# The last numerators' block split over the two column halves of TensorE, and the numerators' PSUM tiles in other banks

## The chip, the cores and the metric

The kernel runs on one core of a Trainium2 chip. The metric is the device time of one execution in microseconds (us), as the median of several executions. The engines are named as in the profile: PE is TensorE, PEld its weight loads, DVE VectorE, ACT ScalarE, POOL GpSimd (PoolE), SP SyncE with its DMA queue.

## The reference

There are 2048 tokens of width 576 and 32 heads of 18 columns. Two linear attentions run over the same input; a gate that depends on the token mixes their outputs.

```python
x = A_x
g = sigmoid((x * gate_w).sum(-1, keepdims=True))
return g * A(x) + (1 - g) * B(x)

# A: q, k, v = x @ wqkv;  phi(t) = where(t > 0, t + 1, exp(t)) + 1e-6
# B: q, k, v = x @ wqkv;  q and k times w_phi, head by head;  phi(t) = [softmax(t), softmax(-t)]
# both, head by head:
kv  = phi(k)^T v                    # summed over all tokens
z   = phi(k) summed over all tokens
o   = (phi(q) kv) / (phi(q) z + 1e-6)
out = o (heads side by side) @ wo
```

All is float32. The phi(q) kv of B is called the numerators below: its denominators and the gate are multiplied into phi(q) ahead of it.

## The kernel before

**Three stages.** First come A's keys and values, then (to about 296 us) B's. Both take the tokens in 8 pairs of tiles of 128 rows and gather the sums kv and z. A's kv is multiplied into its output weights, so A's rows need no numerators of their own. The last stage goes over the 8 pairs once more. Iteration `i` of its loop (L1292) holds the q products of pair `i + 1` (`q_units`, seven products by Strassen's scheme, into double banks), the transposes of pair `i` (`tr_units`), and the numerators (`num`) and the output (`out_units`) of pair `i - 1`. The numerators of the eight groups stand in iterations 1 to 8.

**Transposes.** For each tile of a pair, the odd one first, TensorE transposes four 128x128 pieces of A's normalised rows (`f2` of `norm_a`, profile name `row`) into one bank. ScalarE rounds them to the high part `ath`, VectorE subtracts that from the bank and writes the low part `atl` (profile: `at`). The fourth piece is columns 448 to 575 of the row. Only columns 512 to 575 of it, transposed rows 64 to 127, are used; rows 0 to 63 are overwritten later. Then the 11 blocks of B's rows (`late`) are transposed into three banks, and ScalarE copies them into `uT`, 118 x 11 x 256 for the pair.

**Numerators.** Heads go in threes: 11 blocks of up to 64 columns. A block's matmul (`kb[:, b]` against `uT[:, b]`) gives 64 rows by 256 tokens. Blocks 2n and 2n+1 are put in the lower and the upper 64 columns of the array; two such pairs fill one PSUM bank of 512 columns, so the blocks take a first tile (0 to 3), a second (4 to 7) and half of a third (8 to 10). Block 10 stands alone in the lower half; its 64 rows go into the free rows 0 to 63 of `ath[:, 3]` and `atl[:, 3]`, so that one operand of 128 rows holds both A's last rows and block 10. The other blocks go into `vo` (`oh` high, `ol` low), again by a ScalarE copy and a VectorE subtraction for each tile.

**Output.** `out_units` makes each tile's rows in two halves of 288 columns. A half is 27 matmuls into one ordinary bank: nine of A's rows, fifteen of the `vo`, and last three of the shared operand `ath[:, 3]`, `atl[:, 3]`. Its weights stand in `WOt`, loaded by `load_out` from DRAM (`WO_d`, `MA_d`) over SP's queue.

**PSUM.** All tiles come from pools of two buffers: `pq`, double banks for the products; `tr`, one bank each, for transposes; `bk`, one "ordinary" bank each, for output and other sums. The numerators before take both `tr` banks and one `bk` (`num`, L1228), and in the last two groups a `pq` and a `tr`.

**The order of the work.** Nothing is issued as it is written. `Plan` records every operation, and so in the profile all have the line L354. `weigh` gives each an estimated cost by its engine and size; `order` gives TensorE's operations due times in the order of the code, and the others due times by what they feed, which includes the operations that wait for a PSUM or SBUF buffer to come free; `run` goes through a modelled time and takes on each engine, among the operations ready, the one due first. A change of a tile's pool therefore changes the order on all engines. All matmuls of `num` are one piece and are not torn apart. A matmul with 64 output rows or fewer has another mode in this model, and a change of mode a price.

Of the kernel before, what the change touches and what calls it, by code (L numbers as in the profile page):

```python
# [13 lines left out]
F32R = mybir.dt.float32r  # L14
AF = mybir.ActivationFunctionType
ALU = mybir.AluOpType
AX = mybir.AxisListType

P = 128
S, D, H, DH = 2048, 576, 32, 18  # L20
NT = S // P
# [7 lines left out]
UB = 6 * DH + 10  # L29
NB = len(GRP3)  # L30
# [328 lines left out]
def tile_gated_mix(ctx, tc, xT, wAk, wAv, wBv, wAq, wkT, wqT, phi, woA, woB, out):  # L359
    nc = tc.nc  # L360
    plan = Plan()
    V, A, G, PE, SP = [Engine(plan, k, x) for k, x in (("DVE", nc.vector), ("ACT", nc.scalar), ("POOL", nc.gpsimd),
                                                       ("PE", nc.tensor), ("SP", nc.sync))]
# [3 lines left out]
    wk = Pool(plan, "wk", ctx.enter_context(tc.tile_pool(name="wk", bufs=2)), 2)  # L367
# [4 lines left out]
    def r(ap):  # L372
        return ap.bitcast(F32)
# [7 lines left out]
    def tr_tile():  # L381
        return ps.tile([P, 512], F32, name="tr")
# [12 lines left out]
    def bank_tile():  # L395
        return ps.tile([P, 512], F32, name="bk")

    def row_tile():
        return wk.tile([P, 612], F32, name="row", bufs=8)

    def uw_tile():
        return wk.tile([P, 2, D], F32, name="uw")

    def op_tile(w=D):
        return wp.tile([P, 4, w], F32R, name="op", bufs=11)

    def tail_tile(w=D):
        return wp.tile([P, 2, w], F32R, name="tail")
# [39 lines left out]
    kb = cst.tile([UB, NB, 64], F32, name="kb")  # L448
# [248 lines left out]
    def ub_blocks(ub):  # L697
        return ub[:, :UB * 10].rearrange("p (b c) -> p b c", c=UB)
# [101 lines left out]
    def plain(x, w1, w2, k, t, make):  # L800

        acc = make()
        xa, xb, xt = (x["11"], x["12"], x["t1"]) if t == 0 else (x["21"], x["22"], x["t2"])
        st = op_steps(xa, WA[w1]) + op_steps(xb, WA[w2]) + tail_steps(xt, TA[:, k])
        return acc, [(acc, hf, HG, st, lo, hi) for lo, hi in ((0, 3), (3, 6), (6, 9), (9, 12), (12, 14)) for hf in range(2)]
# [31 lines left out]
    for t in range(2):  # L837
        v, s = plain(x, 12, 3, 1, t, two_banks if t == 0 else pq_tile)
# [5 lines left out]
    for t in range(2):  # L844
        k, s = plain(x, 1, 2, 0, t, two_banks if t else pq_tile)
# [4 lines left out]
    for t in range(2):  # L850
        v, s = plain(x, 12, 3, 1, t, two_banks if t else pq_tile)
# [61 lines left out]
    WO_d = dr.tile([P, 6, 2, D], F32, name="wod")  # L913
# [133 lines left out]
    for n in range(NT // 2):  # L1047
        done, pend = pend, []
        if n % 2:
            lo = wk.tile([P, 2, D], F32, name="st", bufs=1) if n == 1 else area[0][:, :2 * D].rearrange("p (s n) -> p s n", s=2)  # L1050
# [24 lines left out]
    def load_out(k, at):  # L1075
        t = op_tile() if k < 4 else tail_tile()
        WOt[k] = t
        plan.first = at
        if k < 3:
            SP.dma_start(r(t).rearrange("p (i s) n -> p i s n", i=2), WO_d[:, 2 * k:2 * k + 2])  # L1080
        elif k == 3:
            to = r(t).rearrange("p (i s) n -> p i s n", i=2)
            SP.dma_start(to[:126], MA_d[:252].rearrange("(g p) s n -> p g s n", g=2))
            SP.dma_start(to[126:], MA_d[570:574].rearrange("(g p) s n -> p g s n", g=2))
        else:
            SP.dma_start(r(t[:126]), MA_d[252:378])
            SP.dma_start(r(t[126:]), MA_d[574:])

    WOt = {}

    def WO(s, i):
        return WOt[i // 2][:, 2 * (i % 2) + s]
# [36 lines left out]
    def norm_a(t, f, ub):  # L1129
        zw = row_tile()[:, :D]  # L1130
        G.tensor_tensor(zw, f[:, :D], z_a, op=ALU.mult)
        den = sm.tile([P, 32], F32, name="den")
        V.tensor_reduce(den, zw.rearrange("p (h d) -> p h d", d=DH), op=ALU.add, axis=AX.X)
        V.tensor_scalar(den, den, EPS, gate[:, 0, at_row(t):at_row(t) + 1], op0=ALU.add, op1=ALU.mult)
        V.reciprocal(den, den)

        f2 = row_tile()
        blocks = f2[:, :384].rearrange("p (g c) -> p g c", g=3)
        G.tensor_tensor(blocks[:, :, :126].rearrange("p g (k d) -> p g k d", d=DH),
                        f[:, :378].rearrange("p (g k d) -> p g k d", g=3, d=DH),  # L1140
                        den[:, :21].rearrange("p (g k) -> p g k", g=3)[:, :, :, None].to_broadcast([P, 3, GH, DH]), op=ALU.mult)
        G.tensor_tensor(f2[:, 384:582].rearrange("p (k d) -> p k d", d=DH), f[:, 378:D].rearrange("p (k d) -> p k d", d=DH),
                        den[:, 21:, None].to_broadcast([P, 11, DH]), op=ALU.mult)
        A.activation(blocks[:, :, 126:], f2[:, 576:582].rearrange("p (g c) -> p g c", g=3), AF.Copy)
        A.activation(ub_blocks(ub)[:, :, 108:], f2[:, 384:484].rearrange("p (b c) -> p b c", c=10), AF.Copy)
        A.activation(ub[:, UB * 10 + 72:UB * NB], f2[:, 484:530], AF.Copy)
        return f2

    def norm_b(t, uw, rs, ub, engs):
# [17 lines left out]
    def at_row(t):  # L1167
        return 2 * pairs[t // 2] + t % 2
# [49 lines left out]
            A.activation(uT[:UB, 4 * q:4 * q + nb, c], p1[:UB, :P * nb].rearrange("p (j n) -> p j n", n=P), AF.Copy)  # L1218
            yield

    def num(uT, at, last):
        ath, atl = at
        oh, ol = ot = [wk.tile([P, KT, 256], F32R, name="vo") for _ in range(2)]
        if last:
            q = pq_tile()
            pms = [q[:, 0], q[:, 1], tr_tile()]
        else:
            pms = [tr_tile(), tr_tile(), bank_tile()]  # L1228
        with plan.piece():
            for b in range(NB):  # L1230
                a, k = b % 2, b // 2 % 2
                PE.matmul(pms[b // 4][64 * a:64 * a + 64, 256 * k:256 * k + 256], kb[:, b, :], uT[:UB, b, :], start=True, stop=True,
                          skip_group_check=True)
        for m, p1 in enumerate(pms):
            j = 2 * m
            n = 2 if j < 4 else 1
            src = p1[:, :256 * n].rearrange("p (j n) -> p j n", n=256)
            A.activation(oh[:, j:j + n], src, AF.Copy)
            V.tensor_tensor(ol[:, j:j + n], src, r(oh[:, j:j + n]), op=ALU.subtract)
            if n == 1:  # L1240
                A.activation(ath[:64, 3], p1[:64, 256:], AF.Copy)
                V.tensor_tensor(atl[:64, 3], p1[:64, 256:], r(ath[:64, 3]), op=ALU.subtract)
        return ot

    def out_units(t, blk):
        ath, atl = blk["at"]
        oh, ol = blk["ot"]
        c = slice(P * (t % 2), P * (t % 2) + P)
        osb = row_tile()[:, :D]
        dst = out[P * at_row(t):P * at_row(t) + P]  # L1250
        for hf in range(2):
            po = bank_tile()
            cc = slice(HB * hf, HB * hf + HB)
            srcs = [(ath, atl, m, 6 + m) for m in range(3)] + [(oh, ol, j, j) for j in range(KT)] + [(ath, atl, 3, 5)]
            st = []
            for hi, lo, j, i in srcs:
                st += [(hi[:, j, c], WO(0, i)), (hi[:, j, c], WO(1, i)), (lo[:, j, c], WO(0, i))]
            for i, (l, w) in enumerate(st):
                PE.matmul(po[:, :HB], l, w[:, cc], start=(i == 0), stop=(i == len(st) - 1))
            A.activation(osb[:, cc], po[:, :HB], AF.Copy)  # L1260
            if t >= NT - 2:
                SP.dma_start(dst[:, cc], osb[:, cc])
            if hf == 0:
                yield
        if t < NT - 2:
            SP.dma_start(dst, osb)
        yield
# [16 lines left out]
    uT = wide_tile(0, [NB, 256])  # L1284
# [7 lines left out]
    for i in range(NT // 2 + 1):  # L1292
        while norms:
            norms.pop(0)()
        cur, prev = blocks[i], blocks[i - 1]
        seqs = []
        if i and i <= NT // 2:
            prev["ot"] = num(uT, prev["at"], i >= NT // 2 - 1)
        if i + 1 < NT // 2:
            x = x_fetch(pairs[i + 1])  # L1300
            if i == 0:
                load_out(3, x["dma"])
                load_out(4, x["dma"])
            if i == 1:
                for k, m in enumerate((1, 4, 6)):
                    load_out(k, x["dma"][m:m + 1])
            uws = [extra_uw if i == 0 else uw_tile(), uw_tile()]
            seqs.append((7, .7, q_units(i + 1, x, uws, row_tile)))
        ts = (2 * i + 1, 2 * i)
        if i < NT // 2:  # L1310
            at = at_tile([2, 4, 256], F32R)
            cur["at"] = (at[:, 0], at[:, 1])
            seqs.append((8, 1, chain(*[tr_units(t, cur["at"], uT) for t in ts])))
        if i:
            seqs.append((4, 1, chain(*[out_units(t, prev) for t in (2 * i - 1, 2 * i - 2)])))
        merge(*seqs)
# [86 lines left out]
```

## Time and profile before

| | |
|---|---|
| median of 3 runs | 561.73 us (561.55 to 562.09) |
| profiled execution, its own time | 561.08 us |
| its span | 559.4 us |
| granted TensorE clock | 1.0 |
| data moved by DMA | 96.22 MB, 172 GB/s over the span |
| starts of the second to the eighth numerators | 347.28, 381.94, 415.98, 450.01, 484.06, 518.10, 539.84 us |
| TensorE in 340 to 360 us | busy 19.33 of 20 us |
| TensorE in 360 to 380 us | busy 20.00 of 20 us |

Times in the trace count from the start of the span. A row of the timeline has the start, the duration, the engine, the operation with its tiles (out<-in), for matmuls the part of the array, shape, type and count, and in brackets the idle time before it and what ended it. A row of the groups has the busy time, the mean of one in ns, and the idle time before. A row of the page's first part has an engine's busy time.

### The profile page before, as it was taken

The page shows a single profiled execution, that of the slowest core. Times are in us where ns is not written, and L with a number is a line of the kernel's source. Part 1 is how long each engine was busy: PE and PEld are TensorE (multiplying, and loading weights), DVE is VectorE, ACT ScalarE, POOL GpSimd, SP SyncE. Part 2 cuts the span into 40 slices and gives each one's busy share as a digit, 9 for nine tenths or more (in the row PEclk, how much of TensorE's full clock was granted, in tenths as well). Part 3 has the DMA queues.
Part 4 walks back from the last instruction along what each step waited for, and adds up shares of the span by engine and source line. Part 5 has one row for each costly group of instructions (what it writes and reads, how often), then busy time and mean ns, then how long its engine had stood idle before and what let it go on. Part 6 is the DMA issues. An engine that isn't in the chain of part 4 may idle for free.

```text
span 559.4 us, 11694 instructions
## 1 busy us (share of the span) xinstructions
PE 550.0 (98%) x4584; PEld 525.1 (94%) x4584; DVE 423.3 (76%) x674; ACT 287.1 (51%) x602; POOL 243.7 (44%) x218
## 2 busy tenths in 40 slices
PE   9999999999999999999999989999999999999997
PEld 8999999999999978999998989998999989899897
DVE  5882678933887898998889998769597795978810
ACT  6766677655645544543355645445453544535421
POOL 6584486533783523353138764224152332424200
PEclk9999999999999999999999999999999999999999
DMA  8839677976769566887559622132322213100001
GB/s 290 283 121 332 212 261 260 353 236 256 259 243 374 169 218 217 246 248 269 209 184 312 233 88 69 51 105 68 107 79 86 98 49 117 52 2 22 33 33 42
DMA packets 38625, 96.22 MB, mean 172 GB/s; under 512 B 4198, under 2 KB 7782, under 8 KB 37034
## 3 DMA queue, kind: packets, MB, share of 16 engines
q1 hardware_dynamic: 38570, 95.47, 50.3%
q8 instruction: 36, 0.59, 0.4%
q14 instruction: 19, 0.16, 0.1%
HBM read 59.64 MB, written 36.70 MB: 172 GB/s over the span
## 4 chain that ended last, share of the span: by engine, by line
PE 77%; DVE 14%; POOL 3%; ACT 2%; issue 2%; DMA 1%; SPq 0%; POOLq 0%; ACTq 0%; DVEq 0%
PE pq L354 32%; PE tr L354 24%; PE bk L354 22%; DVE row L354 3%; DVE den L354 2%; DVE dd L354 2%; DVE ss L354 2%; DVE mm L354 1%; DVE at L354 1%; POOL late L354 1%; ACT row L354 1%; DMA at<-xT 1%; POOL row L354 1%; DVE rs L354 1%; DVE uw L354 1%
## 5 line engine op out<-in xcount | busy, mean ns | idle before, releaser
L354 PE MATMUL pq<-op,x 128*128 128x288 f32 (+1 forms) x636 | 102.4, 296 | 0.0
L354 PEld LDWEIGHTS pq<-op,x 128*128 128x128 f32 x636 | 90.1, 188 | 0.9 <-issue 0.4
L354 PE MATMUL bk<-op,vo 128*128 128x288 f32 x480 | 71.0, 297 | 0.0
L354 PE MATMUL pq<-tail,x 128*128 128x288 f32 (+1 forms) x308 | 67.2, 301 | 0.4 <-POOL x L354 0.4
L354 PEld LDWEIGHTS bk<-op,vo 128*128 128x128 f32 x480 | 65.8, 188 | 0.2 <-DVE vo L354 0.2
L354 PE MATMUL pq<-op,xp 128*128 128x288 f32 (+1 forms) x336 | 54.0, 297 | 0.0
L354 PE MATMUL bk<-op,at 128*128 128x288 f32 x288 | 51.3, 301 | 0.0
L354 PEld LDWEIGHTS pq<-tail,x 128*128 128x128 f32 x308 | 49.1, 188 | 1.9 <-POOL x L354 0.6
L354 POOL TENSOR_TENSOR row<-row,z_a 128x576 f32<-128x576 f32 x16 | 22.9, 1429 | 63.2 <-issue 35.7
L354 ACT ACTIVATE row<-bk 128x288 f32<-128x288 f32 x38 | 15.6, 410 | 64.3 <-PE bk L354 64.3
L354 ACT ACTIVATE row<-tr 128x288 f32<-128x288 f32 (+1 forms) x74 | 30.1, 408 | 34.8 <-PE tr L354 33.6
L354 PEld LDWEIGHTS pq<-op,xp 128*128 128x128 f32 x336 | 47.5, 188 | 0.2
L354 ACT ACTIVATE row<-row,epsc 128x576 f32<-128x576 f32 x54 | 41.9, 776 | 11.0 <-DVE row L354 10.1
L354 POOL TENSOR_TENSOR row<-row,den 128x378 f32<-128x378 f32 (+1 forms) x32 | 24.6, 788 | 47.8 <-DVE den L354 39.4
L354 DVE TENSOR_REDUCE ss<-uw 128x64 f32<-128x1152 f32 x23 | 31.0, 1350 | 19.0 <-ACT uw L354 18.4
L354 PEld LDWEIGHTS bk<-op,at 128*128 128x128 f32 x288 | 41.7, 189 | 0.4 <-issue 0.4
L354 POOL TENSOR_TENSOR x<-at,x 128x384 fp32r<-128x384 f32 (+2 forms) x35 | 31.6, 907 | 16.5 <-ACT x L354 15.0
L354 ACT ACTIVATE uw<-uw 128x1152 f32<-128x1152 f32 x23 | 26.8, 1164 | 21.3 <-DVE uw L354 11.1
L354 DVE TENSOR_TENSOR row<-row,pq 128x576 f32<-128x576 f32 (+1 forms) x30 | 22.5, 750 | 19.1 <-ACT row L354 14.3
L354 PE MATMUL tr<-op,xv 128*128 128x288 f32 (+1 forms) x204 | 33.6, 301 | 0.0
L354 ACT ACTIVATE uT<-tr 118x512 f32<-118x512 f32 (+1 forms) x48 | 25.9, 558 | 14.6 <-PE tr L354 14.5
L354 POOL TENSOR_TENSOR uw<-uw,rs 128x1152 f32<-128x1152 f32 x8 | 18.0, 2250 | 32.5 <-DVE rs L354 26.3
(206 smaller groups left out, 1263.3 us busy)
## 6 DMA issues: line engine op xcount, KB each, us to landing
xp<-s0x SPq DMA_DIRECT2D x12, 512.0 KB
at<-xT SPq DMA_DIRECT2D x18, 320.0 KB
x<-x1x SPq DMA_DIRECT2D x12, 384.0 KB
x<-s2x SPq DMA_DIRECT2D x12, 384.0 KB
s0x<-xp SPq DMA_DIRECT2D x8, 512.0 KB
out<-row SPq DMA_DIRECT2D x14, 288.0 KB
op<-wb SPq DMA_DIRECT2D x3, 1152.0 KB
wod<-op SPq DMA_DIRECT2D x3, 1152.0 KB
```

The costliest lines, as they stand in the source:

```text
L354: fn(*[a.real() if isinstance(a, View) else a for a in args], **{k: v.real() if isinstance(v, View) else v for k, v in kw.items()})
```

## The change

Block 10 now stands in both halves of the array: two matmuls of 128 columns (tokens) each in place of one of 256. The odd tile of a pair, which has the upper 128 tokens, finds its block 10 in PSUM rows 64 to 127, and so in rows 64 to 127 of `ath[:, 3]`. A's last rows must then stand in rows 0 to 63 there: PoolE copies columns 512 to 575 of an odd tile's normalised row to 448 to 511 ahead of the transposes, and the last three output matmuls of an odd tile take weights with the two halves exchanged, which two further loads (`load_swap`) bring into the tile `st` once. The copy and the subtraction of block 10 are made for each half.

Independent of this, the second of the three numerator tiles comes from the ordinary banks in place of the transposes' from the second group on; the first group and the last two keep the banks they had.

```diff
+    def load_swap():
+        t = WOt["swap"] = wk.tile([P, 2, D], F32R, name="st", bufs=1)
+        for a in range(2):
+            SP.dma_start(r(t[64 * a:64 * a + 64]), WO_d[64 - 64 * a:P - 64 * a, 5])
...
     def norm_a(t, f, ub):
...
+        if t % 2:
+            G.tensor_copy(f2[:, 448:512], f2[:, 512:576])
         return f2
...
-    def num(uT, at, last):
+    def num(uT, at, last, first):
...
-            pms = [tr_tile(), tr_tile(), bank_tile()]
+            pms = [tr_tile(), tr_tile() if first else bank_tile(), bank_tile()]
         with plan.piece():
-            for b in range(NB):
+            for b in range(NB - 1):
                 a, k = b % 2, b // 2 % 2
                 PE.matmul(pms[b // 4][64 * a:64 * a + 64, 256 * k:256 * k + 256], kb[:, b, :], uT[:UB, b, :], start=True, stop=True,
                           skip_group_check=True)
+            for a in range(2):
+                PE.matmul(pms[2][64 * a:64 * a + 64, 256:384], kb[:, NB - 1, :], uT[:UB, NB - 1, P * a:P * a + P], start=True, stop=True,
                           skip_group_check=True)
...
             if n == 1:
-                A.activation(ath[:64, 3], p1[:64, 256:], AF.Copy)
-                V.tensor_tensor(atl[:64, 3], p1[:64, 256:], r(ath[:64, 3]), op=ALU.subtract)
+                for a in range(2):
+                    h, c = slice(64 * a, 64 * a + 64), slice(P * a, P * a + P)
+                    A.activation(ath[h, 3, c], p1[h, 256:384], AF.Copy)
+                    V.tensor_tensor(atl[h, 3, c], p1[h, 256:384], r(ath[h, 3, c]), op=ALU.subtract)
...
     def out_units(t, blk):
...
-                st += [(hi[:, j, c], WO(0, i)), (hi[:, j, c], WO(1, i)), (lo[:, j, c], WO(0, i))]
+                w0, w1 = [WOt["swap"][:, s] if i == 5 and t % 2 else WO(s, i) for s in range(2)]
+                st += [(hi[:, j, c], w0), (hi[:, j, c], w1), (lo[:, j, c], w0)]
...
-            prev["ot"] = num(uT, prev["at"], i >= NT // 2 - 1)
+            prev["ot"] = num(uT, prev["at"], i >= NT // 2 - 1, i == 1)
...
             if i == 1:
                 for k, m in enumerate((1, 4, 6)):
                     load_out(k, x["dma"][m:m + 1])
+                load_swap()
```

TensorE's order at the third numerators (381.94 us in the profile before). `tr<-uT,kb` and `bk<-uT,kb` are numerator blocks by the bank that they go to, `pq<-op,xu` and `pq<-op,x` q products, `tr<-ident,row` the transposes of A's next rows, and `bk<-op,at`, `bk<-tail,at`, `bk<-op,vo` the first output half. Before:

```order
L354 MATMUL tr<-ident,late 118x128 x3
L354 MATMUL pq<-op,xu 128x288 x8
L354 MATMUL tr<-uT,kb 64x256 x8
L354 MATMUL bk<-uT,kb 64x256 x3
L354 MATMUL pq<-op,xu 128x288 x4
L354 MATMUL bk<-op,at 128x288 x6
L354 MATMUL bk<-tail,at 128x288 x3
L354 MATMUL bk<-op,vo 128x288
L354 MATMUL tr<-ident,row 128x128 x4
L354 MATMUL bk<-op,vo 128x288 x14
```

And now, with `bk<-st,at` for the swapped weights:

```order
L354 MATMUL tr<-ident,late 118x128 x3
L354 MATMUL pq<-op,xu 128x288 x8
L354 MATMUL tr<-uT,kb 64x256 x4
L354 MATMUL bk<-uT,kb 64x256 x6
L354 MATMUL bk<-uT,kb 64x128 x2
L354 MATMUL pq<-op,xu 128x288 x4
L354 MATMUL tr<-ident,row 128x128 x4
L354 MATMUL pq<-op,x_4581 128x288 x6
L354 MATMUL bk<-op,at 128x288 x6
L354 MATMUL bk<-tail,at 128x288 x3
L354 MATMUL bk<-op,vo 128x288 x15
L354 MATMUL bk<-st,at 128x288 x3
```

The transposes of the next rows have moved ahead of the output, six q matmuls too, and the output half is no longer torn.

VectorE's order at the same numerators: `vo<-tr,vo` and `vo<-bk,vo` are the subtractions of the numerator tiles, `at<-bk,at` those of block 10, `at<-tr,at` that of A's transposed rows. Before:

```order
L354 TENSOR_REDUCE den<-row 128x32
L354 TENSOR_TENSOR vo<-tr,vo 128x512 x2
L354 TENSOR_TENSOR vo<-bk,vo 128x256
L354 TENSOR_TENSOR at<-bk,at 64x256
L354 TENSOR_SCALAR den<-den,gate 128x32
L354 RECIPROCAL den<-den 128x32
L354 TENSOR_TENSOR row<-uw,z_b 128x576
L354 TENSOR_TENSOR at<-tr,at 128x4x128
L354 TENSOR_REDUCE dd<-row 128x32
```

Now:

```order
L354 TENSOR_REDUCE den<-row 128x32
L354 TENSOR_TENSOR vo<-bk,vo 128x512
L354 TENSOR_TENSOR vo<-tr,vo 128x512
L354 TENSOR_TENSOR vo<-bk,vo 128x256
L354 TENSOR_TENSOR at<-bk,at 64x128
L354 TENSOR_SCALAR den<-den,gate 128x32
L354 RECIPROCAL den<-den 128x32
L354 TENSOR_TENSOR row<-uw,z_b 128x576
L354 TENSOR_TENSOR at<-tr,at 128x4x128
L354 TENSOR_TENSOR at<-bk,at 64x128
L354 TENSOR_REDUCE dd<-row 128x32
```

The ordinary bank's tile is subtracted first, and the second half of block 10 stands behind the subtraction of the next transposes.

VectorE's order ahead of the second numerators' first subtraction: `dd`, `den` and `rs` are the small sums and factors of B's denominators, `row<-uw,z_b` a product with z. Before:

```order
L354 TENSOR_TENSOR dd<-dd,rs 128x64
L354 SCALAR_TENSOR_TENSOR den<-dd 128x32
L354 RECIPROCAL den<-den 128x32
L354 SCALAR_TENSOR_TENSOR rs<-den,gate,rs 128x64
L354 TENSOR_TENSOR late<-uw,rs 128x10x54 x2
L354 TENSOR_TENSOR late<-uw,rs 128x72
L354 TENSOR_REDUCE den<-row 128x32
L354 TENSOR_SCALAR den<-den,gate 128x32
L354 RECIPROCAL den<-den 128x32
L354 TENSOR_TENSOR vo<-tr,vo 128x512 x2
```

Now:

```order
L354 TENSOR_TENSOR late<-uw,rs 128x72
L354 SCALAR_TENSOR_TENSOR row<-row 128x576
L354 TENSOR_TENSOR row<-uw,z_b 128x576
L354 TENSOR_REDUCE dd<-row 128x32 x2
L354 TENSOR_REDUCE den<-row 128x32
L354 TENSOR_SCALAR den<-den,gate 128x32
L354 RECIPROCAL den<-den 128x32
L354 RECIPROCAL rs<-ss 128x64
L354 TENSOR_TENSOR dd<-dd,rs 128x64
L354 SCALAR_TENSOR_TENSOR den<-dd 128x32
L354 RECIPROCAL den<-den 128x32
L354 TENSOR_TENSOR vo<-bk,vo 128x512
```

A product with z, its reduction and the chain up to the reciprocal of the next tile now stand ahead of the subtraction.

More of the change, by code (lines that the diff above doesn't have):

```diff
@@ L1227, in num @@
         else:
-            pms = [tr_tile(), tr_tile(), bank_tile()]
+            pms = [tr_tile(), tr_tile() if first else bank_tile(), bank_tile()]
         with plan.piece():
-            for b in range(NB):
+            for b in range(NB - 1):
                 a, k = b % 2, b // 2 % 2
                 PE.matmul(pms[b // 4][64 * a:64 * a + 64, 256 * k:256 * k + 256], kb[:, b, :], uT[:UB, b, :], start=True, stop=True,
+                          skip_group_check=True)
+            for a in range(2):
+                PE.matmul(pms[2][64 * a:64 * a + 64, 256:384], kb[:, NB - 1, :], uT[:UB, NB - 1, P * a:P * a + P], start=True, stop=True,
                           skip_group_check=True)
```

## The prediction

> **What bounds the kernel now.** I read the page first: how busy each engine is, and the chain that ended last.
>
> ```profile
> PE 550.0 (98%) x4584; PEld 525.1 (94%) x4584; DVE 423.3 (76%) x674; ACT 287.1 (51%) x602; POOL 243.7 (44%) x218
> ...
> PE 77%; DVE 14%; POOL 3%; ACT 2%; issue 2%; DMA 1%; SPq 0%; POOLq 0%; ACTq 0%; DVEq 0%
> ```
>
> TensorE is busy for 550.0 of 559.4 us and carries 77% of the chain. So a change counts if it shortens TensorE's stream or changes the few places where TensorE stands still. Next I read TensorE's timeline around one of the eight numerator groups, the third. The start time comes first, then the duration; an x16 stands for 8 matmuls, each issued in two records.
>
> ```profile
> 381.94 1.95 PE L354 MATMUL tr<-uT,kb 118*64 118x256 f32 x16
> 383.71 1.03 PE L354 MATMUL bk<-uT,kb 118*64 118x256 f32 x6
> 384.67 0.81 PE L354 MATMUL pq<-op,xu 128*128 128x288 f32 x4
> 385.32 0.95 PE L354 MATMUL bk<-op,at 128*128 128x288 f32 x6
> 386.11 0.56 PE L354 MATMUL bk<-tail,at 128*128 128x288 f32 x3
> 386.51 0.29 PE L354 MATMUL bk<-op,vo 128*128 128x288 f32 x1
> 386.85 0.63 PE L354 MATMUL tr<-ident,row 128*128 128x128 f32 x4
> 387.23 2.10 PE L354 MATMUL bk<-op,vo 128*128 128x288 f32 x14
> ...
> 389.57 0.96 PE L354 MATMUL pq<-op,x 128*128 128x288 f32 x6
> ...
> 391.69 0.60 PE L354 MATMUL tr<-ident,late 128*118 128x128 f32 x4
> ```
>
> Eight blocks take 383.71 - 381.94 = 1.77 us, 0.44 per pair of blocks: a pair's two matmuls run side by side in the two column halves. The three blocks of the second row take 384.67 - 383.71 = 0.96, so the last block, alone in its half, costs about 0.96 - 0.44 = 0.52 with the way back to the whole array. The transposes at 386.85 start 0.34 after the matmul before them, where 0.13 is usual (six from 385.32 to 386.11): 0.2 us is lost. The weight loads say the same, and VectorE's timeline says why.
>
> ```profile
> 386.82 0.42 PEld L354 LDWEIGHTS tr<-ident,row 128*128 128x128 f32 x4 [0.25 <-issue]
> ```
>
> ```profile
> 383.82 1.62 DVE L354 TENSOR_TENSOR late<-uw,rs 128x540 f32<-128x540 f32 x3
> 385.36 0.74 DVE L354 TENSOR_REDUCE den<-row 128x32 f32<-128x576 f32 x1
> 386.02 1.28 DVE L354 TENSOR_TENSOR vo<-tr,vo 128x512 fp32r<-128x512 f32 x2
> ...
> 387.55 0.40 DVE L354 TENSOR_TENSOR at<-bk,at 64x256 fp32r<-64x256 f32 x1
> ```
>
> VectorE is busy without a gap until it subtracts the first two numerator tiles from 386.02 on; the first of these ends near 386.66, and 0.16 later the transposes get its bank. So the release stands at 4.88 us after the group's start (386.82 - 381.94), set by VectorE's queue and not by TensorE. The longer stops of TensorE in this stage, and the start of the second group:
>
> ```profile
> 302.65 1.09 PE L354 MATMUL tr<-ident,late 128*118 128x128 f32 x8 [0.63 <-POOL late L354]
> ...
> 325.08 0.66 PE L354 MATMUL tr<-ident,row 128*128 128x128 f32 x4 [1.16 <-DVE vo L354]
> 333.96 1.09 PE L354 MATMUL tr<-ident,late 128*118 128x128 f32 x8 [0.32 <-POOL late L354]
> ...
> 347.28 1.95 PE L354 MATMUL tr<-uT,kb 118*64 118x256 f32 x16
> ...
> 352.67 0.63 PE L354 MATMUL tr<-ident,row 128*128 128x128 f32 x4 [0.67 <-DVE vo L354]
> ...
> 522.41 0.54 PE L354 MATMUL tr<-ident,late 128*118 128x128 f32 x3 [0.79 <-DVE at L354]
> ```
>
> **The last block in two halves.** Two matmuls of 128 columns, one in each array half, replace one of 256. The trace has no 64-wide matmul of 128 columns; the nearest are those that gather the k-v sums, mostly 108 columns wide, also alternating between the halves:
>
> ```profile
> 281.75 2.31 PE L354 MATMUL bk<-at,vo 128*55 128x108 f32 x44
> 283.98 1.08 PE L354 MATMUL tr<-op,xv 128*128 128x288 f32 x6
> ```
>
> That is 2.23/44 = 0.051 us per record. Scaled by 128/108 it is 0.060, and four records take 0.24 where the lone block streams for about 0.43 to 0.44 (a pair's time): I take 0.2 off each group, bounds 0 (the halves do not overlap) and 0.22 (exactly half a pair). TensorEngine Tiling (Array Packing) in the Trainium skill, section Performance Considerations, gives column tiling up to 2x for a stationary width of at most 64; by this alone the sum would be 8 x 0.2 = 1.6 us less.
>
> **The banks, third to sixth group.** From the second group on, the numerators hold one bank of the transposes and both ordinary banks. The transposes of the next rows therefore have a free bank and lose their wait; the output's first tile, which used to start right behind the group, now needs an ordinary bank that VectorE must first empty. The new order puts four transposes and six q matmuls in front of it and has VectorE subtract the ordinary bank's tile first. Nothing on VectorE before that subtraction is moved in this group, so the release stays at 4.88. TensorE's arrival: the group 2.73 - 0.2 = 2.53 (384.67 - 381.94), four q matmuls 0.65, four transposes 0.38 (387.23 - 386.85), six q matmuls about 0.8: 4.36. It waits 0.5 us. Before, at the same release, it had done the group, four q and ten output matmuls (0.65 + 10 x 0.133 = 1.98 behind the group); now it has done 0.65 + 0.38 + 0.8 = 1.83 behind it. What is then left is 391.69 - 386.85 = 4.84 in the one and 27 output and 10 q matmuls at 0.133 = 4.92 in the other. So the next transposes come 0.05 to 0.1 us later; I take **+0.05 per group, +0.2 for four**. The saving of the halves drops out, since TensorE waits for the same subtraction anyway. If VectorE were early it would be worth -0.4 each (0.2 of stream and 0.2 of the lost wait), the lower end. PSUM Bottleneck, a section of the same page of the Trainium skill, warns that tiling speeds TensorE but not the emptying of PSUM; the rows above bear it out here, and by it this term is zero or above.
>
> **Smaller evictions.** The last block's two evictions become four of half the width.
>
> ```profile
> L354 DVE TENSOR_TENSOR at<-bk,at 64x256 fp32r<-64x256 f32 x6 | 2.4, 407 | 0.0
> L354 DVE TENSOR_TENSOR row<-bk,row 55x108 f32<-55x108 f32 x2 | 0.5, 264 | 0.0
> L354 DVE TENSOR_TENSOR row<-bk,row 55x36 f32<-55x36 f32 x2 | 0.4, 192 | 0.0
> ...
> L354 ACT ACTIVATE at<-bk 64x256 fp32r<-64x256 f32 x6 | 2.2, 366 | 0.0
> ```
>
> From 192 ns at 36 and 264 at 108 columns, 128 columns cost about 0.28 on VectorE: 0.57 for two in place of 0.41, so +0.16; ScalarE between 0 and +0.37. They lie behind the subtraction that TensorE waits for. One counts: the odd tile's half is subtracted after the next transposes' tile, and the last matmul of the first output tile needs it. That matmul is due at 4.88 + 26 x 0.133 = 8.3 after the group's start. VectorE gets there after 4.08 + 1.2 + 0.33 + 0.28, two small operations (0.5), a product 0.67, the transposes' tile 0.6 and the half itself 0.28 = 7.9. The cover is 0.3 to 0.4 us; beyond it the excess is paid once per group.
>
> **First and second group.** The first keeps its banks: TensorE arrives 0.2 earlier and waits for the same subtraction, so it gains nothing. Behind it the planner has moved the output's rest behind the q matmuls, and VectorE's second subtraction behind a reduction. The second group is decided on VectorE:
>
> ```profile
> 328.26 0.75 DVE L354 TENSOR_TENSOR row<-uw,z_b 128x576 f32<-128x576 f32 x1
> 328.93 1.41 DVE L354 TENSOR_REDUCE dd<-row 128x32 f32<-128x576 f32 x2
> 330.37 0.23 DVE L354 TENSOR_TENSOR dd<-dd,rs 128x64 f32<-128x64 f32 x1
> ...
> 331.24 0.28 DVE L354 SCALAR_TENSOR_TENSOR rs<-den,gate,rs 128x64 f32<-128x64 f32 x1
> ...
> 340.92 1.35 DVE L354 TENSOR_REDUCE ss<-uw 128x64 f32<-128x1152 f32 x1 [1.50 <-ACT uw L354]
> ...
> 342.85 1.55 DVE L354 TENSOR_TENSOR row<-uw,z_b 128x576 f32<-128x576 f32 x1
> ...
> 351.90 1.22 DVE L354 TENSOR_TENSOR vo<-tr,vo 128x512 fp32r<-128x512 f32 x2
> ```
>
> By the new order one more product with z_b (0.67 to the next start), one reduction (0.72) and a chain of three small ones (330.37 to 331.24: 0.87) come before the second group's first subtraction: 2.26 us. The idle 1.50 at 340.92 can take the most of it up, and the product that was stretched to 1.55 may run in 0.75. So the subtraction starts between 351.9 and 352.7, and the output's tile 0.8 later, at 352.7 to 353.5, with as much work done as before at 352.67: 0 to +0.8. If VectorE did not bind, TensorE would come by itself at 347.28 + 4.36 = 351.6, -1.0. I take **+0.2**, near the early end, since the waits on PoolE and ScalarE also move up.
>
> **Copy, swapped weights, last groups.** PoolE's new copies (8 x 128x64) stand behind the two products with z_b:
>
> ```profile
> 377.13 3.37 POOL L354 TENSOR_TENSOR row<-uw,z_b 128x576 f32<-128x576 f32 x2 [0.45 <-ACT uw L354]
> ```
>
> ```profile
> masks.py:197 POOL MEMSET ident<- 128x128 f32 x1 | 0.2, 197 | 0.0
> ```
>
> Between 0.1 and 0.4 us each, by the nearest row 0.2. They end near 380.7, and the transposes that need them come at 385.1: covered by 4 us. Only in the first rows (about 299) TensorE meets the copy; that wait takes the place of the 0.63 at 302.65: **+0.1**, from 0 to 0.3. The two loads of the swapped weights stand on SyncE ahead of this load:
>
> ```profile
> 281.85 0.32 SPq L354 DMA_DIRECT2D x<-s1x  x1
> ```
>
> ```profile
> 300.66 1.36 PE L354 MATMUL bk<-op,x 128*128 128x288 f32 x9
> ```
>
> It lands later by their two issues, some 0.7, with 18 us before the matmuls that read it: nothing. The seventh group's 0.2 goes into the wait at 522.41, which is for a subtraction that comes before: 0. Behind that row TensorE stops no more, so the eighth group keeps its saving: **-0.2**.
>
> Sum: 0.1 + 0.2 + 0.2 + 0 - 0.2 = +0.3. The profiled execution took 561.08 (its span 559.4 and 1.68 around it); 561.4 on it. The runs' median, 561.73, is 0.65 above that execution: **562.0 us**. A measurement of this kernel can tell 0.2%, 1.1 us, from no change.
>
> **Rivals.** *The saving arrives (faster).* VectorE releases the ordinary bank 0.4 us earlier than worked out, or the waits hide elsewhere. Then third to sixth give 4 x -0.4, the second -0.5, the eighth -0.2, with +0.1: -2.2, 559.5. For it: the old waits are all on the transposes' banks, which the change frees. Against it: VectorE's rows have no gap before 386.02. Chance 0.21. The 2x of the tiling page points the same way, though by that page alone it would be -1.6.
>
> *The odd half comes late (slower).* The last matmul of the first output tile stands for the second half's subtraction, queued behind the next transposes' tile. It decides from VectorE reaching it 8.2 us or more after the group's start; my margin is 0.3. At 0.7 later it costs 0.4 in each of the second to sixth groups, +2.0, and with the +0.3: 564.0. For it: these are the fullest stretches of VectorE. Against it: the margin. Chance 0.28.
>
> *The halves do not overlap.* Then each group is as long as before; only the eighth shows it: +0.2, 562.2, within the forecast's class. Chance 0.04.
>
> **How the numbers follow.** The forecast, no change within 1.1 us, has the remaining 0.47, with the overlap rival 0.51. Its own range takes the bounds: -1.0 to +0.8 in the second group, 0 to 0.3 at the copy, about 0.2 per group on the four: 560.8 to 563.0. For 8 in 10 I reach into both others, 560.2 to 563.6. Faster 0.21, same 0.51, slower 0.28.
>
> **What would show it.** Right: the numerators' last four records within 0.3 us; no wait before the transposes of the next rows; a wait of 0.3 to 0.6 at the first output tile in the third to sixth groups, released by VectorE; periods of 34.0 to 34.2 us from group to group. Wrong: no such wait and periods of 33.6 (first rival), or a stop at the first output tile's last matmul (second). A stop in front of the second group's output beyond 0.8, or a late load at 300, would break the sum elsewhere.

## The result and the profile after

The changed kernel takes 563.14 us in the median of 6 runs (562.21 to 563.86), the kernel before 561.64 beside it. The ratio is 1.0031, with a 95% interval of 1.0019 to 1.0042. So it is slower, by 1.5 us between the medians and 1.7 by the ratio. The time lies inside the predicted range of 560.2 to 563.6, but just above the 560.8 to 563.0 that the prediction's own terms allowed, and its likeliest case was no change.

The page after, busy times and the chain that ended last:

```profile
PE 550.8 (98%) x4600; PEld 527.0 (94%) x4600; DVE 425.5 (76%) x682; ACT 287.6 (51%) x610; POOL 249.8 (44%) x226
...
PE 65%; DVE 24%; ACT 4%; issue 3%; POOL 3%; DMA 1%; SPq 0%; POOLq 0%; ACTq 0%; DVEq 0%
```

TensorE has as much work as before within 0.8 us; VectorE's share of the chain has grown from 14% to 24%. TensorE's timeline in the first two groups:

```profile
315.83 1.95 PE L354 MATMUL tr<-uT,kb 118*64 118x256 f32 x16
...
325.69 0.66 PE L354 MATMUL tr<-ident,row 128*128 128x128 f32 x4 [1.38 <-DVE vo L354]
...
331.28 0.40 PE L354 MATMUL bk<-op,vo 128*128 128x288 f32 x1 [1.21 <-DVE vo L354]
...
334.72 1.09 PE L354 MATMUL tr<-ident,late 128*118 128x128 f32 x8 [0.25 <-POOL late L354]
...
349.25 1.08 PE L354 MATMUL tr<-uT,kb 118*64 118x256 f32 x8
...
354.24 1.05 PE L354 MATMUL bk<-op,at 128*128 128x288 f32 x6 [0.42 <-DVE vo L354]
```

The stop of 1.21 us at 331.28 is new. From the first to the second group it now takes 33.42 us (349.25 - 315.83), and took 32.04 (347.28 - 315.24). The matmul that stops reads the first group's third numerator tile. VectorE's timeline after shows when that tile is subtracted, and the row behind it where it stood before:

```profile
326.81 0.68 DVE L354 TENSOR_TENSOR vo<-tr,vo 128x512 fp32r<-128x512 f32 x1
327.40 1.76 DVE L354 TENSOR_TENSOR row<-uw,z_b 128x576 f32<-128x576 f32 x1
329.09 1.40 DVE L354 TENSOR_REDUCE dd<-row 128x32 f32<-128x576 f32 x2
330.41 0.54 DVE L354 RECIPROCAL rs<-ss 128x64 f32<-128x64 f32 x1
330.87 0.35 DVE L354 TENSOR_TENSOR vo<-bk,vo 128x256 fp32r<-128x256 f32 x1
```

```profile
327.39 0.36 DVE L354 TENSOR_TENSOR vo<-bk,vo 128x256 fp32r<-128x256 f32 x1
```

A product and two reductions have come ahead of it (the reciprocal stood ahead of it before too). It starts 15.04 us after the group's start (330.87 - 315.83) in place of 12.15 (327.39 - 315.24). About 1.0 of these 2.9 us is the product's own length: it takes 1.76 here and took 0.75 at 328.26 before. Here PoolE runs a product of its own over the first 1.15 us of it:

```profile
327.38 1.17 POOL L354 TENSOR_TENSOR uw<-row,mm 128x576 f32<-128x576 f32 x1
```

No run took this overlap away.

TensorE around the third group after, and the last two rows as they stood before:

```profile
383.56 1.08 PE L354 MATMUL tr<-uT,kb 118*64 118x256 f32 x8
384.48 1.68 PE L354 MATMUL bk<-uT,kb 118*64 118x256 f32 x16
386.09 0.81 PE L354 MATMUL pq<-op,xu 128*128 128x288 f32 x4
386.74 0.60 PE L354 MATMUL tr<-ident,row 128*128 128x128 f32 x4
387.09 1.04 PE L354 MATMUL pq<-op,x 128*128 128x288 f32 x6
388.28 1.07 PE L354 MATMUL bk<-op,at 128*128 128x288 f32 x6
...
391.57 0.56 PE L354 MATMUL bk<-st,at 128*128 128x288 f32 x3
...
393.28 0.60 PE L354 MATMUL tr<-ident,late 128*118 128x128 f32 x4
...
395.31 0.60 PE L354 MATMUL tr<-ident,late 128*118 128x128 f32 x4
395.89 0.53 PE L354 MATMUL pq<-tail,x 128*128 128x288 f32 x2
```

```profile
393.71 0.60 PE L354 MATMUL tr<-ident,late 128*118 128x128 f32 x4
394.06 0.51 PE L354 MATMUL pq<-tail,x 128*128 128x288 f32 x2
```

Up to the transposes at 395.31 the group runs as before: 395.31 - 383.56 = 11.75 us, before 393.71 - 381.94 = 11.77. Then the next q product comes 0.58 later, before 0.35. The weight loads name both waits of the group:

```profile
388.28 0.83 PEld L354 LDWEIGHTS bk<-op,at 128*128 128x128 f32 x6 [0.38 <-DVE vo L354]
...
395.89 0.30 PEld L354 LDWEIGHTS pq<-tail,x 128*128 128x128 f32 x2 [0.22 <-DVE row L354]
```

The second is the new one. The product opens a new double bank, which comes free when VectorE has added its last content (`row<-row,pq`). VectorE's rows after, and that addition before:

```profile
387.54 0.68 DVE L354 TENSOR_TENSOR vo<-bk,vo 128x512 fp32r<-128x512 f32 x1
...
389.19 0.29 DVE L354 TENSOR_TENSOR at<-bk,at 64x128 fp32r<-64x128 f32 x1
...
391.39 0.27 DVE L354 TENSOR_TENSOR at<-bk,at 64x128 fp32r<-64x128 f32 x1
...
393.55 1.62 DVE L354 TENSOR_TENSOR late<-uw,rs 128x540 f32<-128x540 f32 x3
395.09 0.75 DVE L354 TENSOR_TENSOR row<-row,pq 128x576 f32<-128x576 f32 x1
```

```profile
393.12 0.75 DVE L354 TENSOR_TENSOR row<-row,pq 128x576 f32<-128x576 f32 x1
```

The addition now starts 11.53 us after the group's start (395.09 - 383.56), before 11.18 (393.12 - 381.94). It has no gap before it in either, so it is late by what stands ahead of it in VectorE's queue. From its first numerator subtraction to the addition VectorE takes 7.55 us (395.09 - 387.54), before 7.10 (393.12 - 386.02).

The last two groups, TensorE's timeline; the last row of TensorE before stands in the second fence:

```profile
520.62 1.95 PE L354 MATMUL pq<-uT,kb 118*64 118x256 f32 x16
...
542.28 1.95 PE L354 MATMUL pq<-uT,kb 118*64 118x256 f32 x16
...
557.79 0.56 PE L354 MATMUL bk<-op,at 128*128 128x288 f32 x3
```

```profile
555.55 0.56 PE L354 MATMUL bk<-op,at 128*128 128x288 f32 x3
```

From the eighth group to TensorE's last row it takes 15.51 (557.79 - 542.28), before 15.71: here the split's 0.2 us arrives in full.

The following table gives all kernels of this case. A period is the time from the first numerator matmul of a group to that of the next one. "Last stage" is the time from TensorE's twelve matmuls `bk<-op,xu` (at 296.29 us before, 296.84 after) to its last row. Up to there the orders are the same, but the ten profiled executions reach it at 295.94 to 298.00 us, so the stage is a sharper measure than the span. The medians have the kernel before beside them at 561.64 (change), 561.02 (e1 to e4) and 561.00 (e5 to e8); the expectations below were reckoned from 561.64, so some of their times are 0.6 too high.

| kernel | median us | ratio (95%) | last stage | 1st period | 2nd | 3rd to 6th, sum |
|---|---|---|---|---|---|---|
| before | | | 259.26 | 32.04 | 34.66 | 136.16 |
| change | 563.14 | 1.0031 (1.0019 to 1.0042) | 260.95 | 33.42 | 34.31 | 137.06 |
| e1 split alone | 563.18 | 1.0038 (1.0026 to 1.0051) | 261.89 | 33.42 | 35.36 | 136.97 |
| e2 banks alone | 561.47 | 1.0007 (0.9998 to 1.0017) | 259.55 | 32.04 | 34.58 | 136.56 |
| e3 first block whole | 561.85 | 1.0015 (1.0006 to 1.0023) | 259.87 | 32.04 | 34.71 | 137.05 |
| e4 late products last | 563.84 | 1.0054 (1.0042 to 1.0066) | 261.93 | 33.41 | 34.26 | 138.04 |
| e5 addition first | 561.62 | 1.0011 (1.0002 to 1.0020) | 260.05 | 33.43 | 34.32 | 136.13 |
| e6 release first | 562.52 | 1.0027 (1.0018 to 1.0036) | 260.88 | 33.42 | 34.33 | 136.96 |
| e7 both, first whole | 559.26 | 0.9969 (0.9957 to 0.9980) | 257.42 | 32.05 | 34.74 | 134.51 |
| e8 before, both | 559.97 | 0.9981 (0.9973 to 0.9990) | 258.48 | 32.08 | 34.65 | 135.37 |

### The profile page after: what moved, and what is told of

It reads as the page before. It is cut to its first block, busy times and chain, and to the rows that moved or that the text cites. A ratio compares the mean times of both kernels' runs of the same rounds, so it can differ in the third digit from the quotient of the medians.

```text
span 561.5 us, 11744 instructions
## 1 busy us (share of the span) xinstructions
PE 550.8 (98%) x4600; PEld 527.0 (94%) x4600; DVE 425.5 (76%) x682; ACT 287.6 (51%) x610; POOL 249.8 (44%) x226
## 4 chain that ended last, share of the span: by engine, by line
PE 65%; DVE 24%; ACT 4%; issue 3%; POOL 3%; DMA 1%; SPq 0%; POOLq 0%; ACTq 0%; DVEq 0%
PE pq L354 28%; PE tr L354 20%; PE bk L354 16%; DVE row L354 6%; DVE den L354 4%; DVE dd L354 4%; ACT row L354 2%; DVE mm L354 2%; DVE uw L354 2%; DVE ss L354 2%; POOL late L354 2%; DVE late L354 1%; DVE rs L354 1%; DVE at L354 1%; ACT uw L354 1%
## 5 line engine op out<-in xcount | busy, mean ns | idle before, releaser
L354 PE MATMUL bk<-op,at 128*128 128x288 f32 x240 | 43.0, 304 | 1.0 <-DVE vo L354 0.7
L354 PEld LDWEIGHTS bk<-op,at 128*128 128x128 f32 x240 | 34.4, 189 | 2.4 <-DVE vo L354 2.2
```

The source lines that it names most:

```text
L354: fn(*[a.real() if isinstance(a, View) else a for a in args], **{k: v.real() if isinstance(v, View) else v for k, v in kw.items()})
```

## The experiments

Theory A: the loss comes from the split and by way of VectorE's queue. In the first group the planner, with two evictions in place of one, puts the third subtraction behind a product and two reductions (3.0 us, from 327.40 to 330.41); in the third to sixth groups VectorE reaches the addition that frees a q bank later. Rival B: the banks cost it. Rival C: the copies and the swapped weights do. Rival D: VectorE is full, and only the sum of its work counts. The first four runs take the change apart.

**e1, the split without the banks.**

```diff
-            pms = [tr_tile(), tr_tile() if first else bank_tile(), bank_tile()]
+            pms = [tr_tile(), tr_tile(), bank_tile()]
```

> The block is split in every group (copies, swapped weights and half evictions included), but the numerators keep two transposes' banks and one ordinary bank. Theory A (the loss comes from the split: the planner moves the first group's third subtraction back, and VectorE's longer evictions hold up a q product later in each group): the first period stays at about 33.4 us (32.04 before), third to sixth stay 0.1 to 0.25 above 34.04, the time is 562.8 to 563.3. Rival B (third to sixth lose by the banks, since the output now waits for VectorE): third to sixth come back to 33.8 to 34.05 and the time is 562.0 to 562.4, with the first period still at 33.4.

TensorE's stops in the first and the second group, and VectorE's addition in the third group, which starts at 383.84:

```profile
330.52 0.40 PE L354 MATMUL bk<-op,vo 128*128 128x288 f32 x1 [1.21 <-DVE vo L354]
...
354.58 0.63 PE L354 MATMUL tr<-ident,row 128*128 128x128 f32 x4 [1.58 <-DVE vo L354]
```

```profile
395.37 0.75 DVE L354 TENSOR_TENSOR row<-row,pq 128x576 f32<-128x576 f32 x1
```

As theory A has it: the same stop of 1.21, the same first period, the addition again 11.53 after the start (395.37 - 383.84) and 7.55 after the first subtraction (at 387.82), and third to sixth as long as with the banks. Rival B falls for these. What was not expected is the second period, 35.36: there TensorE stands 1.58 us in front of the transposes. VectorE's first subtraction starts 5.32 us after the group's start there (353.80 - 348.48), before 4.62 (351.90 - 347.28) and in the change 4.31 (353.56 - 349.25); what makes it later without the banks is open. In the change the second period is 1.05 shorter than in e1 (34.31).

**e2, the banks without the split.** From the kernel before:

```diff
-            pms = [tr_tile(), tr_tile(), bank_tile()]
+            pms = [tr_tile(), tr_tile() if first else bank_tile(), bank_tile()]
```

> Only the banks are changed (one transposes' and two ordinary from the second group on); the last block stays whole, as before. Theory A: first period 32.0, third to sixth 34.0 to 34.15, the time 561.4 to 562.0, which can't be told from before. Rival B (the banks cost the 0.2 per group): third to sixth at 34.2 to 34.3, 562.4 to 562.8.

```profile
393.13 0.75 DVE L354 TENSOR_TENSOR row<-row,pq 128x576 f32<-128x576 f32 x1
```

The addition starts 11.19 after the group's start (381.94) and 7.10 after the first subtraction (at 386.03) as in the kernel before, the first period is 32.04, and third to sixth lose 0.1 each. The time can't be told from before. So the banks alone are worth nothing here; beside the split they save 1.05 us in the second period, as e1 shows.

**e3, the first block whole.** In `norm_a` and `out_units` the odd tile of the first pair is left as before, and so are the first group's matmuls and evictions:

```diff
-        if t % 2:
+        if t % 2 and t > 1:
             G.tensor_copy(f2[:, 448:512], f2[:, 512:576])
...
-                w0, w1 = [WOt["swap"][:, s] if i == 5 and t % 2 else WO(s, i) for s in range(2)]
+                w0, w1 = [WOt["swap"][:, s] if i == 5 and t % 2 and t > 1 else WO(s, i) for s in range(2)]
...
-            for a in range(2):
+            for a in range(2 if two else 0):
```

> As changed, but the first group's block stays whole (no copy and no swapped weights for its odd tile); by the orders, everything up to the second group then stands as before. Theory A: the stop of 1.2 us at 331 goes, the first period falls from 33.4 to 32.0 to 32.1; the second may give back up to 0.35 (34.3 to 34.7), third to sixth unchanged at 34.2 to 34.3: 561.8 to 562.2. Rival C (the first period is long because of the copy or the loads of the swapped weights at its start, which stay or come later): 33.4 stays in the first or appears in the second period, 563.0 to 563.3.

TensorE's stops in the first group, now as before:

```profile
325.37 0.65 PE L354 MATMUL tr<-ident,row 128*128 128x128 f32 x4 [1.16 <-DVE vo L354]
...
334.24 1.09 PE L354 MATMUL tr<-ident,late 128*118 128x128 f32 x8 [0.32 <-POOL late L354]
```

The first period is 32.04 again, and the second gives back 0.40 of the 1.38. The loads are still made, so rival C falls for them; the copy of the first pair is gone together with its split. In the planner's order alone, without a run, leaving out the copies, the loads or both keeps the third subtraction where the change put it, and so does putting the two matmuls back into one. Only one eviction in place of two, with all the rest as changed, puts it back to where it stood before. That the planner moves it because of the two evictions is therefore shown; that its place alone makes the 1.38 us is not, since no run moved only that subtraction.

**e4 and e5, what stands ahead of the addition.** A step behind the planner takes single operations further back in its list, here the three products `late<-uw,rs` of the even tile in the second to sixth groups; nothing else moves.

```diff
+    for i in range(2, NT // 2 - 1):
+        at = plan.marks["c22", i + 1]
+        for op in plan.marks["late", 2 * i]:
+            plan.moves.append((op, at))
+            at = op
```

`late` marks the three products and `c22` one of the two additions `row<-row,pq`; e5 has `c1`, the other one, in its place. These kernels are longer, so the helper's line is L364 in them. e4 put the products behind the wrong addition, ten microseconds further back than meant:

> As changed, but on VectorE the three products that make the even tile's scaled rows (late) are moved behind the addition of two q products (row<-row,pq) in the second to sixth groups; nothing else moves on any engine. Theory A: the stop of 0.2 us at the q matmuls some 12.3 us after each group's start goes, third to sixth come to 34.05 to 34.1, the time falls by 0.8 to 1.0 to 562.1 to 562.4. Rival D (the 0.2 is lost elsewhere, at the first output tile or in the array, and would only move): periods stay at 34.2 to 34.3, 562.9 to 563.3.

Its weight load in front of the first output tile of the third group (start 383.82), and VectorE's late products:

```profile
388.92 0.83 PEld L364 LDWEIGHTS bk<-op,at 128*128 128x128 f32 x6 [0.77 <-DVE vo L364]
```

```profile
405.60 1.61 DVE L364 TENSOR_TENSOR late<-uw,rs 128x540 f32<-128x540 f32 x3
```

The stop at the q product is gone from the trace, but the periods are longer, which neither side had said. In the stretch from 405 on, which leads up to the next numerators, the products find too little room: the release that TensorE waits for comes 5.10 us after the start (388.92 - 383.82) in place of 4.72 (388.28 - 383.56). 0.38 more there and 0.22 less at the q product make 0.16, and the third period grew by 0.14 (34.28 to 34.42). So a place on VectorE has a price of its own, which speaks against rival D as well. e5 has them behind the addition that the trace names:

> As changed, but on VectorE the three products that scale the even tile's rows (late) stand behind the first addition of two q products, the one at 395.09 us in the changed profile, in the second to sixth groups. Theory A (that addition frees the double bank for which TensorE stands still 0.22 us, 12.3 us after each group's start): the stop goes, third to sixth come to 34.05 to 34.1, the time is 0.8 to 1.0 lower, 562.0 to 562.4. Rival D (VectorE is full from there to the next numerators, so what it does first does not matter): periods stay at 34.2 to 34.3, 562.9 to 563.3.

VectorE in its third group (start 384.72):

```profile
394.64 0.75 DVE L364 TENSOR_TENSOR row<-row,pq 128x576 f32<-128x576 f32 x1
395.31 1.61 DVE L364 TENSOR_TENSOR late<-uw,rs 128x540 f32<-128x540 f32 x3
```

The addition starts 9.92 after the start, TensorE's stop at the q product is gone, and third to sixth take 136.13, as long as before the change. VectorE does the same work. That this stop is the 0.9 us of the third to sixth groups is shown.

**e6, an earlier release.** In the third to sixth groups the reduction `den<-row` goes behind the subtraction for which the first output tile waits.

```diff
+            plan.moves.append((plan.marks["den", 2 * i], plan.marks["subs", i][1]))
```

> As changed, but in the third to sixth groups the reduction den<-row (0.74 us) stands behind the subtraction of the ordinary bank's numerators in place of ahead of it. Theory A: the wait at the first output tile (0.4 in the weight loads) goes, but the addition that frees the q products' bank stays where it is on VectorE, so the stop 12.3 us after the start grows from 0.2 to about 0.5, and the periods stay at 34.2 to 34.3: 562.9 to 563.4. Rival E (the prediction's first rival: an earlier release is worth what TensorE waited): 33.85 to 34.0, 561.8 to 562.3.

```profile
395.67 0.53 PE L364 MATMUL pq<-tail,x 128*128 128x288 f32 x2 [0.38 <-DVE row L364]
```

TensorE no longer waits at the first output tile, and waits 0.38 at the q product instead (in the weight loads 0.62, up from 0.22). Third to sixth are unchanged. The prediction's first rival would not have arrived by this alone.

**e7 and e8, both.** e7 is e3 with both moves; e8 is the kernel before with both moves and nothing of the change.

> The block whole in the first group and split from the second on, and both of the last two reorderings. Theory A: with both waits gone the split's 0.2 of stream comes through as well, third to sixth at 33.7 to 33.9, the first period 32.0: 1.5 to 2.0 below the version with the first block whole, 559.9 to 560.4, ratio to before 0.997 to 0.999. Rival D: 34.05 or more, 561.0 to 561.8.

> The kernel before with the same two reorderings on VectorE and nothing else. Theory A: the 0.2 us that TensorE loses ahead of the transposes of the next rows goes, third to sixth at 33.8 to 33.9 in place of 34.04, 0.6 to 0.9 below before: 560.1 to 560.5. If it is as fast as the version before this one in the list, the split is worth nothing beside the order. Rival D: 34.04, no change.

TensorE in the third group of e7, from the numerators over the first output tile to the q product, and the numerators in e8:

```profile
383.24 1.08 PE L364 MATMUL tr<-uT,kb 118*64 118x256 f32 x8
...
385.77 0.81 PE L364 MATMUL pq<-op,xu 128*128 128x288 f32 x4
...
387.65 0.95 PE L364 MATMUL bk<-op,at 128*128 128x288 f32 x6
...
394.93 0.51 PE L364 MATMUL pq<-tail,x 128*128 128x288 f32 x2
```

```profile
381.59 1.95 PE L364 MATMUL tr<-uT,kb 118*64 118x256 f32 x16
...
384.33 0.81 PE L364 MATMUL pq<-op,xu 128*128 128x288 f32 x4
```

In neither does TensorE stand still at these places any more. e7 has periods of 33.61 to 33.66, e8 of 33.83 to 33.87, about 0.21 apart, and the numerators take 2.53 us in e7 (385.77 - 383.24) and 2.74 in e8 (384.33 - 381.59). So with the waits gone the split's 0.2 us comes through in the third to sixth groups too, as it does in the eighth of the change. e7 also has the changed banks, and no run has the moves and the banks without the split; the numerators' own time already accounts for the 0.21, so little is left for the banks. e7 is the fastest kernel of this case, 0.9969 of before. More came than expected (2.45 us of the last stage against e3, with 1.5 to 2.0 foreseen): the whole 0.4 of the first wait went, not only a part of it.

## Why the prediction was right in part, and where not

**The halves, right.** With two halves for the last block the third group's numerators take 2.53 us (386.09 - 383.56) in place of 2.73 (384.67 - 381.94), and the eighth group gains 0.20.

**The third to sixth group, right up to 9.7 us, then wrong.** Release 4.88 predicted, 4.72 measured; TensorE's arrival 4.36, measured about 4.33 (387.09 + 6 x 0.133 - 383.56); a wait of 0.5, measured 0.38. The next transposes were to come 0.05 to 0.1 later; they come 0.03 earlier (9.72 after the start, before 9.75). The step that failed is the cover of the smaller evictions: they were sized right (two halves of 0.285 us, by the mean of 12, for one of 0.407: +0.16), but their cover was counted for one reader only, the odd tile's last matmul. What is queued behind them was not followed, and there stands the addition that frees a q bank. It came 0.35 later: the first subtraction came 0.10 earlier, and VectorE needed 0.45 more from there on. By the times from one start to the next, 0.19 of that is the two halves (0.32 and 0.20 for 0.33). Nearly all the rest is that two instructions, the first half and the subtraction of the transposed rows, start 0.12 to 0.13 later behind the one before them than they did; it comes with the split (7.55 in e1, 7.10 in e2), but why is open. TensorE, which had about 0.13 to spare there before (0.35 - 0.22), stopped for 0.22. Term +0.2, measured +0.90 (137.06 - 136.16). The prediction took the section PSUM Bottleneck of TensorEngine Tiling (Array Packing) in the Trainium skill for a bound at zero of this term. The same section of the Trainium skill advises to vectorize PSUM access; the trace agrees as far as one eviction cut in two takes 0.57 us in place of 0.41.

**First and second group, wrong in the first.** The text says that the planner moved the output's rest and a subtraction, and prices only the first release: "it gains nothing". The third tile's subtraction, which moved by 2.9 us, was left out, and so was that nine output matmuls, which TensorE had done ahead of the wait on PoolE's scaled rows (325 to 334 us), now come behind it. Nor did it allow for the product's 1.0 us beside PoolE. Term +0.2 for both groups with -1.0 to +0.8; measured +1.38 and -0.35, together +1.03, outside. The second group by itself was within its bounds. Its own wait, 0.86 to 0.89 us at the first output tile in e3 and e7, was left as it is and is open.

**The rest.** First rows +0.1, measured +0.04 (18.99 in place of 18.95 up to the first numerators); seventh group 0, measured -0.08; eighth -0.2, measured -0.20. The sum was +0.3, and the last stage grew by 1.69: 0.83 too little in the first two groups and 0.70 in the third to sixth. Two terms were short in the same direction, and the time still lies in the range only because that had been widened for both rivals; this is luck and not a confirmed sum. Of the signs named, the short last records, the free transposes and the wait at the first output tile came; the periods of 34.0 to 34.2 did not (34.21 to 34.31).

**The rivals.** The odd half was not late: VectorE was done with it 8.10 us after the start (391.39 + 0.27 - 383.56), and by an estimate from the row at 391.57, two matmuls of 0.133 on, it was needed at 8.28. The prediction had 7.9 and 8.3. So the slower rival had the right engine and the right instructions and named the wrong reader. The halves do overlap, and the saving arrives only in e7.

## What to carry to other kernels

When an instruction on a full queue grows or is cut in two, follow the queue past its own reader to the next instruction that frees a buffer for the bottleneck: cover that was counted for one reader is no cover for those behind. In a changed order, price every operation that now has long ones ahead of it, not only the first that is waited for. A saving in the bottleneck's stream is seen only where no wait follows it: the same 0.2 us was worth nothing in the third to sixth groups, and came in full once VectorE's order had been changed in two places.

## What the runs showed of the hardware

PoolE's copy of 128x64 was priced at 0.2 us. Three of the eight take 0.23 to 0.25, but five take 0.83 to 0.84. Two of PoolE's rows, and the VectorE row that starts with the second:

```profile
345.96 0.24 POOL L354 COPY row<-row 128x64 f32<-128x64 f32 x1 [1.75 <-ACT late L354]
...
382.06 0.83 POOL L354 COPY row<-row 128x64 f32<-128x64 f32 x1
```

```profile
382.05 0.74 DVE L354 SCALAR_TENSOR_TENSOR row<-row 128x576 f32<-128x576 f32 x1
```

In all five long ones (at 382, 416, 451, 485 and 519 us) VectorE began such an instruction within 0.01 us of the copy, and the copy ended about 0.1 us after it. SBUF — State Buffer in the Trainium skill, section SBUF: two separate sides, says that the two engines share a port pair which one of them holds for a whole instruction; the rows agree, though no run took the overlap away. VectorE's product at 327.40, longer by 1.0 us beside PoolE's, fits as well. One row fits less well: the short copy at 345.96 overlaps a VectorE instruction of two operands (345.81 to 346.10) and is no longer for it. The long copies cost nothing here, since no transpose waits for them. TensorE waits only for the first, short one:

```profile
299.96 0.33 PE L354 MATMUL tr<-ident,row 128*128 128x128 f32 x1 [0.19 <-POOL row L354]
```

The stop behind that row falls from 0.63 us (302.65 before) to 0.38, so hardly anything is lost.
